# Emitting the weight conversion of the first batch by sums of engine times

## The chip, the cores and the metric

The kernel runs on one core of one Trainium2 chip. The metric is the device time of one execution in microseconds (us). Before the change it is 1535.84 us, the median of three runs (1533.26 to 1537.35).

## What is computed

The reference, cut to what matters (float32 tensors of attention; the four weight matrices arrive as float64):

```python
def sm_attn(qq, kk, vv):
    s = scale * np.matmul(qq, kk.transpose(0, 1, 3, 2))
    a = np.exp(s - np.max(s, axis=-1, keepdims=True))
    return np.matmul(a / (np.sum(a, axis=-1, keepdims=True) + 1e-09), vv)
# q, k, v: (8, 8, 576, 64); p: (8, 8, 32, 64)
p_packed = sm_attn(p, k, v)
out = sm_attn(q, p_packed, p_packed)
x = out.transpose(0, 2, 1, 3).reshape(4608, 512)
h = x @ w_in                      # (512, 2048)
x = (h - np.tanh(h)) @ w_out      # (2048, 512)
r = np.maximum(x @ w_in2, 0.0)
out = (s * (r * r) + b) @ w_out2
```

## The kernel before, in words

The attention and the first MLP run batch by batch; the second MLP follows and is not touched. For each batch the packed keys give z, which is the attention's last product folded into w_in: one z per column block c of 512 of w_in (four blocks, `make_z`, L421), and a, the softmax of the second attention, one per half of the batch's tokens (`second_stage`, L624). A step j is one of 16 blocks of 128 rows of d_ff: `mm1` (L456) multiplies z by a for block j, `act_pe` or `act1` forms h - tanh(h), and `mm2` (L492) adds the product with row block j of w_out. Numbers are split into a high and a low float32r part, so each product is three matmuls. The first batch goes in four parts of eight steps j: half 0 and half 1 with j from 0 to 7, then both halves with j from 8 to 15. Its first three parts use `act_pe`, which keeps the subtraction of tanh on TensorE; the fourth and all later batches use `act1`, which does it on VectorE.

The weights are converted from float64 to float32 on the chip during the first batch. `to_f32` (L114) does it in five instructions: an absolute value on ScalarE (L119), a clamp, a shift and two bit merges on VectorE (L121, L123, L126, L129). `w1_steps(c, i)` converts half i of column block c of w_in (128 x 1024 numbers). `wo1_steps(j)` converts row block j of w_out (128 x 512), and then splits it: a cast on ScalarE (L138) and a subtraction (L140), on GpSimd for j below 12, else on VectorE. Each is a generator that yields after each instruction.

Every engine works its own instructions in the order in which the program emits them, and DMAs wait in the queue of the engine that issues them. The order is made by hand. `first_weights` (L687) lists groups of generators; `in_turn` (L634) runs the groups one after another, the members of one group in turns (`both`, L527), and starts the generators of the next group after 13 steps of a group, or four for each of its members if that is fewer. `attention` (L777) goes on from there with the attention of the next batches. `slot` (L806) is called at six places of a step j, between matmuls, and takes steps out of that generator: before the last row block of w_out is converted, 5, 3, 4 or 1 sixths of a step in the four parts (SLOTS), and after each `mm1` 6, 5, 4 or 1 more (AFTER). After that it is one step a slot, and four more a step j (CATCH_UP) until a of batch 1 is there. `until` (L648) takes steps until something that the next instruction needs has been emitted: z before `mm1`, row block j before `mm2`.

Loads of float64 weights go out on SyncE's queue (SP). `load_wo1` (L586) puts row blocks 8 to 11 into the place of blocks 4 to 7, so each waits for the subtraction of one of these; a column block's load waits for a free one of nine large buffers (`take_turn`, L561). The loads of k, v and q of batch 1 and later are issued by GpSimd (`load_k` L161, `load_v` L173, `load_q` L231): 16, 2 and 16 DMAs; those of k and q have pieces of 128 bytes, 288 in each DMA. `second_loads` (L629) issues the first of them. `load_p` (L226) is on SP. A second generator (`second_weights`, L703) converts the weights of the second MLP later on, a step every third slot.

Of the kernel before, what the change touches and what calls it, by code (L numbers as in the profile page):

```python
# [18 lines left out]
def pack_attention_two_mlps(ctx, tc, q, k, v, p, w_in1, w_out1, w_in2, w_out2, s_in, b_in, out):  # L19
# [36 lines left out]
    AFTER, SLOTS = (6, 5, 4, 1), (5, 3, 4, 1)  # L56
    ON_PE = 3
    AHEAD, CATCH_UP, FIRST_W = 13, 4, range(23, 33)
# [55 lines left out]
    def to_f32(x, src, t):  # L114


        low, high = words(src)
        tf = t.bitcast(F32)
        nc.scalar.activation(tf, high.bitcast(F32), AF.Abs)  # L119
        yield  # L120
        nc.vector.tensor_scalar(out=tf, in0=tf, scalar1=EXP_LO, scalar2=EXP_HI, op0=ALU.max, op1=ALU.min)  # L121
        yield
        nc.vector.tensor_scalar(out=t, in0=t, scalar1=3, scalar2=0x3FFFFFF8, op0=ALU.logical_shift_left,  # L123
                                op1=ALU.bitwise_and)
        yield
        nc.vector.scalar_tensor_tensor(out=t, in0=high, scalar=-0x40000000, in1=t, op0=ALU.bitwise_and,  # L126
                                       op1=ALU.bitwise_or)
        yield
        nc.vector.scalar_tensor_tensor(out=x.bitcast(I32), in0=low, scalar=29, in1=t,  # L129
                                       op0=ALU.logical_shift_right, op1=ALU.bitwise_or)  # L130
        yield
# [29 lines left out]
    def load_k(b, g):  # L161
        for hp in range(2):
            h0 = 4 * g + 2 * hp
            t = apool.tile([P, 2, C, 32], F32, tag="kr", name=f"k_{b}_{g}_{hp}", bufs=2)
            rows = k[b, h0:h0 + 2].rearrange("h (r a n) d -> a r h n d", a=2, n=C)
            for a in range(2):
                for u in range(2):
                    p0 = (2 * a + u) * 32
                    for e in range(2):
                        nc.gpsimd.dma_start(out=t[p0:p0 + 32, e], in_=rows[a][:, e, :, u * 32:u * 32 + 32])  # L170
            k_t[b, g, hp] = t

    def load_v(b, g):  # L173

        t = apool.tile([P, 4, CT * D], F32, tag="v", name=f"v_{b}_{g}", bufs=1)
        src = v[b, 4 * g:4 * g + 4].rearrange("h (r c) d -> r h (c d)", c=C)
        nc.gpsimd.dma_start(out=t[:R], in_=src[:, :, :CT * D])
        nc.gpsimd.dma_start(out=t[R:, :, :(C - CT) * D], in_=src[:, :, CT * D:])
        v_t[b, g] = t.rearrange("r h (c d) -> r h c d", c=CT)
# [51 lines left out]
    def load_q(b, hf):  # L231
        for g in range(G):
            for hp in range(2):
                h0 = 4 * g + 2 * hp
                t = apool.tile([P, HB // 32, 32], F32, tag="qr", name=f"q_{b}_{hf}_{g}_{hp}", bufs=4)
                for u in range(2):
                    for e in range(2):
                        src = q[b, h0 + e, hf * HB:(hf + 1) * HB, u * 32:u * 32 + 32]
                        p0 = (2 * e + u) * 32
                        nc.gpsimd.dma_start(out=t[p0:p0 + 32], in_=src.rearrange("(n r) d -> r n d", r=32))  # L240
# [286 lines left out]
    def both(gens):  # L527
        gens = list(gens)
        while gens:
            for g in list(gens):  # L530
                try:
                    next(g)
# [3 lines left out]
                yield  # L536
# [14 lines left out]
    with tc.manual_schedule():  # L551
# [82 lines left out]
        def in_turn(*groups):  # L634

            groups = [[call_late(g) for g in group] for group in groups]
            for n, group in enumerate(groups):
                for i, _ in enumerate(both(group)):
                    yield
                    if i == min(AHEAD, 4 * len(group)) and n + 1 < len(groups):  # L640
                        for g in groups[n + 1]:
                            next(g)

        def call_late(f):
            g, *a = f
            yield from g(*a)

        def until(key, gen):  # L648
            forced.append(key)
            while key not in done:  # L650
                next(gen)
# [35 lines left out]
        def first_weights():  # L687
            yield from in_turn(
                [(w1_steps, 1, 0)], [(w1_steps, 1, 1)],
                [(wo1_steps, 0), (wo1_steps, 1)],  # L690
                [(first_z, 1), (wo1_steps, 2), (wo1_steps, 3)],
                [(wo1_steps, 4), (wo1_steps, 5)],
                [(second_stage, 0, 1), (wo1_steps, 6), (wo1_steps, 7)],
                [(w1_steps, 2, 0)], [(w1_steps, 2, 1)],
                [(wo1_steps, 8), (wo1_steps, 9)],
                [(first_z, 2), (wo1_steps, 10), (wo1_steps, 11)],
                [(w1_steps, 3, 0)], [(w1_steps, 3, 1)],
                [(wo1_steps, 12), (wo1_steps, 13), (second_loads,)],
                [(first_z, 3), (wo1_steps, 14), (wo1_steps, 15)])
# [106 lines left out]
        def slot():  # L806
# [20 lines left out]
        for b in range(B):  # L827
# [4 lines left out]
            for hf, js in parts:  # L832
# [10 lines left out]
                for j in js:  # L843
# [14 lines left out]
                    if on_pe:  # L858
                        next(t)
                    between = None  # L860
# [453 lines left out]
```

## Time and profile before

| what | value |
|---|---|
| median of three runs | 1535.84 us |
| the profiled execution | 1534.77 us, of which the span from first to last instruction is 1533.0 us |
| granted clock of TensorE, mean | 0.986 |
| busy, share of the span | TensorE 96%, its weight loads 91%, VectorE 70%, ScalarE 49%, GpSimd 24% |
| first batch, its four parts | 45.7, 34.8, 29.3 and 33.0 us |

Parts are cut at the first `mm1` of each. In the table a busy TensorE includes time in which a matmul stands in its pipeline; the weight loads are the closer measure of its pace. A wait in the trace is the idle time of an engine ahead of an instruction, with what ended it.

### The profile page before, as it was taken

How to read it: one execution, taken by the hardware profiler on the slowest of the kernel's cores; microseconds unless marked ns; L12 is line 12 of the kernel's file. 1: busy time of each engine (PE TensorE's matmuls, PEld its weight loads, DVE VectorE, ACT ScalarE, POOL GpSimd, SP SyncE). 2: the span in 40 equal slices, each digit the busy share in tenths (PEclk: the TensorE clock that was granted, in tenths of full speed). 3: DMA queues.
4: the chain of work that ended last, by engine and by line, in shares of the span. 5: the costliest groups of instructions: out<-in, count | busy, mean ns of one | idle time of the engine just before them, and what ended most of it. 6: DMA issues, size and time to landing. Idle time of an engine off the chain costs nothing.

```text
span 1533.0 us, 28189 instructions
## 1 busy us (share of the span) xinstructions
PE 1473.5 (96%) x10548; PEld 1387.5 (91%) x10548; DVE 1066.9 (70%) x2032; ACT 756.7 (49%) x1466; POOL 368.8 (24%) x584
## 2 busy tenths in 40 slices
PE   6689899999999999999999999999998999999998
PEld 3578698998988989888999999999998999999998
DVE  4784887878787797876554777777776865565563
ACT  3465344544444444443334656656666655454442
POOL 0238462534527275543001000000031000000000
PEclk8799999999999999999999999999999999999999
DMA  9656454554634444342427465465498886676673
GB/s 211 195 144 156 109 151 124 141 145 125 169 95 129 114 133 124 86 108 81 157 90 297 173 245 225 177 257 215 186 317 322 251 252 185 220 239 195 222 236 83
DMA packets 250394, 271.64 MB, mean 177 GB/s; under 512 B 113040, under 2 KB 188816, under 8 KB 250256
## 3 DMA queue, kind: packets, MB, share of 16 engines
q1 hardware_dynamic: 226880, 222.42, 45.3%
q0 software_dynamic: 22848, 46.83, 11.5%
q8 instruction: 83, 1.36, 0.4%
q10 hardware_dynamic: 528, 0.59, 0.1%
q14 instruction: 55, 0.45, 0.1%
HBM read 161.61 MB, written 108.13 MB: 176 GB/s over the span
## 4 chain that ended last, share of the span: by engine, by line
PE 82%; DVE 8%; DMA 3%; ACT 2%; issue 2%; SPq 1%; POOL 1%; ACTq 0%; DVEq 0%; POOLq 0%
PE acc L499 21%; PE h L464 11%; PE Y L1252 10%; PE Y L1035 9%; PE Z L1252 7%; PE X L1035 6%; PE X L1252 6%; PE Z L1035 6%; PE zp L367 2%; DMA w1s<-in_moe_w_in_dram 1%; SPq L194 1%; DVE gl L135 1%; DMA wo1s<-in_moe_w_out_dram 1%; PE pv L339 1%; PE s L270 1%
## 5 line engine op out<-in xcount | busy, mean ns | idle before, releaser
L499 PE MATMUL acc<-gh,wo 128*128 128x288 f32 x2040 | 419.7, 297 | 4.3 <-POOL wo L140 4.3
L499 PEld LDWEIGHTS acc<-gh,wo 128*128 128x128 f32 x2040 | 330.7, 189 | 4.6 <-POOL wo L140 4.5
L499 PE MATMUL acc<-gl,wo 128*128 128x288 f32 x1020 | 310.1, 304 | 6.7 <-ACT wo L138 2.8
L472 ACT ACTIVATE t<-h 128x288 f32<-128x288 f32 x232 | 95.3, 411 | 299.7 <-PE h L464 255.6
L499 PEld LDWEIGHTS acc<-gl,wo 128*128 128x128 f32 x1020 | 193.1, 189 | 33.9 <-issue 18.7
L464 PE MATMUL h<-a2h,z 128*128 128x288 f32 x1024 | 214.7, 297 | 1.5 <-ACT z L445 1.5
L939 DVE TENSOR_TENSOR x<-B,x 128x768 fp32r<-128x768 f32 x158 | 147.2, 950 | 82.8 <-ACT x L1186 68.0
L473 DVE TENSOR_TENSOR t<-h,t 128x288 f32<-128x288 f32 x232 | 104.2, 449 | 135.5 <-ACT t L472 134.8
L464 PE MATMUL h<-a2l,z 128*128 128x288 f32 x512 | 161.0, 314 | 8.8 <-ACT gl L483 3.4
L464 PEld LDWEIGHTS h<-a2h,z 128*128 128x128 f32 x1024 | 165.7, 190 | 2.9 <-ACT z L445 1.7
L240 POOL DMA_DIRECT2D q<-in_q_dram x224 | 135.2, 612 | 133.0 <-DVE qT L374 113.7
L1035 PE MATMUL Y<-x,w 128*128 128x384 f32 x864 | 160.6, 339 | 4.8 <-DVE g L939 4.1
L1035 PEld LDWEIGHTS Y<-x,w 128*128 128x128 f32 x864 | 152.9, 190 | 5.5 <-DVE g L939 4.4
L1252 PE MATMUL Y<-x,w 128*128 128x384 f32 x864 | 153.2, 335 | 0.7 <-DVE s L939 0.7
L1252 PEld LDWEIGHTS Y<-x,w 128*128 128x128 f32 x864 | 150.3, 188 | 1.0 <-DVE s L939 1.0
L170 POOL DMA_DIRECT2D k<-in_k_dram x224 | 136.1, 615 | 50.2 <-DVE kT L290 40.7
L464 PEld LDWEIGHTS h<-a2l,z 128*128 128x128 f32 x512 | 97.7, 191 | 26.3 <-issue 6.8
L1186 ACT CAST x<-B 128x768 fp32r<-128x768 f32 x116 | 94.0, 833 | 47.1 <-DMA B<-g 30.6
L1035 PE MATMUL X<-x,w 128*128 128x384 f32 x576 | 108.0, 336 | 0.0
L1035 PE MATMUL Z<-x,w 128*128 128x384 f32 x576 | 107.9, 336 | 0.0
L135 DVE TENSOR_TENSOR gl<-t,gh 128x288 fp32r<-128x288 f32 x231 | 107.0, 463 | 0.0
L1252 PE MATMUL X<-x,w 128*128 128x384 f32 x576 | 102.6, 336 | 0.0
(176 smaller groups left out, 2269.6 us busy)
## 6 DMA issues: line engine op xcount, KB each, us to landing
g<-g SPq DMA_DIRECT2D x196, 384.0 KB, 3.5
B<-g SPq DMA_DIRECT2D x116, 384.0 KB, 4.5
w<-w_d POOLq DMA_DIRECT2D x28, 512.0 KB, 6.0
B<-x2t SPq DMA_DIRECT2D x24, 384.0 KB, 5.7
g<-s SPq DMA_DIRECT2D x24, 384.0 KB, 2.8
out_dram<-g SPq DMA_DIRECT2D x192, 48.0 KB, 1.8
x2t<-xs SPq DMA_DIRECT2D x15, 576.0 KB, 3.7
w1s<-in_moe_w_in_dram SPq DMA_DIRECT2D x32, 256.0 KB, 8.2
```

Of the source, the lines that this page charges most:

```text
L135: (eng or nc.vector).tensor_tensor(out=lo, in0=x, in1=hi.bitcast(F32), op=ALU.subtract)
L170: nc.gpsimd.dma_start(out=t[p0:p0 + 32, e], in_=rows[a][:, e, :, u * 32:u * 32 + 32])
L240: nc.gpsimd.dma_start(out=t[p0:p0 + 32], in_=src.rearrange("(n r) d -> r n d", r=32))
L367: nc.tensor.matmul(ps[e][i * M:(i + 1) * M, :rhs(i).shape[-1]], pblk[b][r, h // 4, h % 4 * M:h % 4 * M + M], rhs(i)[r], start=True, stop=True)
L464: nc.tensor.matmul(h[:, :HB], zt[:, zi, g, f0:f0 + P], a[:, g], start=(n == 0), stop=(n == 3 * G - 1))
L472: nc.scalar.activation(t, h[:, :HB], AF.Tanh)
L473: nc.vector.tensor_tensor(out=t, in0=h[:, :HB], in1=t, op=ALU.subtract)
L499: nc.tensor.matmul(acc[m][:, :HB], w[:, m * P:(m + 1) * P], x, start=(j == js[0] and i == 0), stop=(j == js[-1] and i == 2))
L939: self.nc.vector.tensor_tensor(out=o, in0=a, in1=b, op=op)
L1035: self.nc.tensor.matmul(bank[:, f, :self.TH], w[:, f, a, kt], x[:, b, kt], start=(p in ("P1", "P5", "P6") and m == 0), stop=(m == 5), skip ...
L1186: self.nc.scalar.copy(self.xs[(7 * self.NBK + n) % self.XS][:, 0], self.ready[0])
L1252: nc.tensor.matmul(bank[:, ft, :T], w[:, kk, u, ft], x[:, v, kk], start=first and p in ("P1", "P5", "P6"), stop=last, skip_group_check=True)
```

## The change

Every yield of `to_f32` now gives a number, an estimate of the time on VectorE; a yield without one counts as half a STEP (0.17). Two sums are kept: `clock[0]` grows by SLOT with every slot, `clock[1]` by what is emitted, and a slot emits until the second is ahead of the first by LEAD. AFTER, SLOTS, AHEAD and CATCH_UP go. This goes on until a of batch 1 is emitted, so it paces the first attention steps of batch 1 too; after that it is one step a slot. A group takes the first step (the absolute value) of the next group's conversions when each of its members has had a step. The order of groups is changed: row blocks 0 to 3 of w_out stand ahead of column block 1 of w_in; z(1) goes with row blocks 4 and 5; `second_loads` goes from the group of row blocks 12 and 13 to its own place ahead of column block 2. The loads of k, v and q of batch 1 are issued on SP instead of GpSimd.

```diff
-    AFTER, SLOTS = (6, 5, 4, 1), (5, 3, 4, 1)
+    STEP, SLOT, LEAD = 0.34, (0.7, 0.52, 0.52, 0.42), 1.0
-    AHEAD, CATCH_UP, FIRST_W = 13, 4, range(23, 33)
+    FIRST_W = range(23, 33)
...
+        one = STEP * (len(t.shape) - 1)
         nc.scalar.activation(tf, high.bitcast(F32), AF.Abs)
-        yield
+        yield 0.0
...
-        yield
+        yield one
...
-        yield
+        yield 2 * one
...
-                        nc.gpsimd.dma_start(out=t[p0:p0 + 32, e], in_=rows[a][:, e, :, u * 32:u * 32 + 32])
+                        (nc.gpsimd if b > 1 else nc.sync).dma_start(out=t[p0:p0 + 32, e], in_=rows[a][:, e, :, u * 32:u * 32 + 32])
...
         def in_turn(*groups):
 
-            groups = [[call_late(g) for g in group] for group in groups]
+            groups = [[(f, f(*a)) for f, *a in group] for group in groups]
             for n, group in enumerate(groups):
-                for i, _ in enumerate(both(group)):
-                    yield
-                    if i == min(AHEAD, 4 * len(group)) and n + 1 < len(groups):
-                        for g in groups[n + 1]:
-                            next(g)
+                for i, cost in enumerate(both([g for _, g in group])):
+                    yield cost
+                    if i == len(group) and n + 1 < len(groups):
+                        for f, g in groups[n + 1]:
+                            if f in (w1_steps, wo1_steps):
+                                next(g)
+
+        clock = [0.0, 0.0]
+
+        def step(gen):
+            cost = next(gen)
+            clock[1] += STEP / 2 if cost is None else cost
 
         def until(key, gen):
             forced.append(key)
-            while key not in done:
-                next(gen)
+            if key not in done:
+                while key not in done:
+                    step(gen)
+                clock[0] = max(clock[0], clock[1])
             forced.pop()
...
-                [(w1_steps, 1, 0)], [(w1_steps, 1, 1)],
-                [(wo1_steps, 0), (wo1_steps, 1)],
-                [(first_z, 1), (wo1_steps, 2), (wo1_steps, 3)],
-                [(wo1_steps, 4), (wo1_steps, 5)],
+                [(wo1_steps, 0)], [(wo1_steps, 1)],
+                [(wo1_steps, 2), (wo1_steps, 3)],
+                [(w1_steps, 1, 0)], [(w1_steps, 1, 1)],
+                [(first_z, 1), (wo1_steps, 4), (wo1_steps, 5)],
                 [(second_stage, 0, 1), (wo1_steps, 6), (wo1_steps, 7)],
+                [(second_loads,)],
                 [(w1_steps, 2, 0)], [(w1_steps, 2, 1)],
-                [(wo1_steps, 8), (wo1_steps, 9)],
-                [(first_z, 2), (wo1_steps, 10), (wo1_steps, 11)],
+                [(first_z, 2), (wo1_steps, 8), (wo1_steps, 9)],
+                [(wo1_steps, 10), (wo1_steps, 11)],
                 [(w1_steps, 3, 0)], [(w1_steps, 3, 1)],
-                [(wo1_steps, 12), (wo1_steps, 13), (second_loads,)],
-                [(first_z, 3), (wo1_steps, 14), (wo1_steps, 15)])
+                [(first_z, 3), (wo1_steps, 12), (wo1_steps, 13)],
+                [(wo1_steps, 14), (wo1_steps, 15)])
...
-            if ("wo", NF - 1) not in done:
-                n = SLOTS[part[0]]
-                for _ in range(ticks[0] * n // 6 - (ticks[0] - 1) * n // 6):
-                    next(fill)
+            if ("wo", NF - 1) in done and ticks[0] % 3 == 1:
+                next(more, None)
+            if ("a", 1, 0) in done:
+                next(fill, None)
                 return
-            if ticks[0] % 3 == 1:
-                next(more, None)
-            next(fill, None)
+            clock[0] += SLOT[part[0]]
+            while clock[1] <= clock[0] + LEAD and ("a", 1, 0) not in done:
+                step(fill)
...
-                    if ("wo", NF - 1) not in done:
-                        for _ in range(AFTER[part[0]]):
-                            next(fill)
-                    elif ("a", 1, 0) not in done:
-                        for _ in range(CATCH_UP):
-                            next(fill)
...
                     if on_pe:
                         next(t)
+                    else:
+                        clock[1] += 2 * STEP
```

The same choice of queue stands in `load_v` (two DMAs) and `load_q`; `both` hands the numbers through.

## Rows read from the trace of the kernel before

**Rows 1.** The page: its first line, and part 1.

```profile
span 1533.0 us, 28189 instructions
...
PE 1473.5 (96%) x10548; PEld 1387.5 (91%) x10548; DVE 1066.9 (70%) x2032; ACT 756.7 (49%) x1466; POOL 368.8 (24%) x584
```

**Rows 2.** Busy time by stage: parts 0 to 3 of the first batch, and a later stretch.

```profile
core 0: us, PE busy (x) PEld busy (x) DVE busy (x) ACT busy (x) POOL busy (x), PEclk, DMA share, GB/s
39.00:84.70 45.70, 33.44 (x177) 26.93 (x177) 32.80 (x58) 23.27 (x49) 14.01 (x8) 0.78 0.59 182
84.70:119.50 34.80, 29.50 (x202) 24.14 (x203) 32.46 (x45) 21.63 (x47) 15.17 (x19) 1.00 0.57 149
119.50:148.80 29.30, 28.88 (x252) 25.73 (x253) 13.32 (x32) 16.22 (x45) 26.57 (x45) 1.00 0.72 173
148.80:181.80 33.00, 29.54 (x272) 22.01 (x271) 23.96 (x62) 13.73 (x38) 16.66 (x28) 1.00 0.44 113
190.00:310.00 120.00, 119.58 (x1073) 109.67 (x1073) 99.97 (x267) 57.10 (x154) 61.41 (x102) 1.00 0.53 142
```

**Rows 3.** DVE in order of time: start us, us, line, tiles, count [idle before].

```profile
51.38 0.76 DVE L121 TENSOR_SCALAR t<-t 128x512 f32<-128x512 f32 x2
...
53.92 1.29 DVE L129 SCALAR_TENSOR_TENSOR wo1s<-wo1s,t 128x512 int32<-128x512 int32 x2
64.21 0.43 DVE L121 TENSOR_SCALAR t<-t 128x512 f32<-128x512 f32 x1 [9.00 <-ACT t L119]
```

**Rows 4.** DVE in order of time, from second_stage(0,1) to column block 3.

```profile
70.42 0.47 DVE L389 STREAM_TRANSPOSE t<-s 128x288 f32<-128x288 f32 x1
...
85.75 0.69 DVE L121 TENSOR_SCALAR w<-w 128x1024 f32<-128x1024 f32 x1
...
87.20 1.23 DVE L126 SCALAR_TENSOR_TENSOR w<-w1s,w 128x1024 int32<-128x1024 int32 x1
88.46 1.22 DVE L129 SCALAR_TENSOR_TENSOR w<-w1s,w 128x1024 int32<-128x1024 int32 x1
...
104.69 0.69 DVE L121 TENSOR_SCALAR w<-w 128x1024 f32<-128x1024 f32 x1 [1.12 <-ACT w L119]
...
107.18 2.22 DVE L126 SCALAR_TENSOR_TENSOR w<-w1s,w 128x1024 int32<-128x1024 int32 x1
```

**Rows 5.** PE in order of time: mm1 (h), z's products (zp), scores (s).

```profile
66.69 0.40 PE L464 MATMUL h<-a2h,z 128*128 128x288 f32 x1 [1.51 <-ACT z L445]
...
92.48 2.17 PE L367 MATMUL zp<-w,pblk 64*32 64x512 f32 x16
...
119.50 0.40 PE L464 MATMUL h<-a2l,z 128*128 128x288 f32 x1 [0.92 <-ACT gl L483]
...
125.40 0.51 PE L464 MATMUL h<-a2l,z 128*128 128x288 f32 x1
...
167.96 0.71 PE L367 MATMUL s<-qT,pblk 64*32 64x288 f32 x14 [0.78 <-DVE z L435]
...
180.15 1.69 PE L367 MATMUL zp<-w,pblk 64*32 64x512 f32 x16 [2.46 <-DVE z L435]
```

**Rows 6.** ACT in order of time: absolute values, and the first Exp of stage1.

```profile
63.50 1.24 ACT L119 ACTIVATE t<-wo1s 128x512 f32<-128x512 f32 x2
...
103.53 1.13 ACT L119 ACTIVATE w<-w1s 128x1024 f32<-128x1024 f32 x1
...
134.77 0.41 ACT L310 ACTIVATE e<-s,nm 128x160 f32<-128x160 f32 x1 [1.89 <-DVE nm L302]
```

**Rows 7.** SP's queue in order of time: issues of DMAs, us from first to last.

```profile
72.00 10.44 SPq L594 DMA_DIRECT2D wo1s<-in_moe_w_out_dram  x4
82.49 5.78 SPq L148 DMA_DIRECT2D w1s<-in_moe_w_in_dram  x8
...
1222.78 3.92 SPq L1218 DMA_DIRECT2D out_dram<-g  x8
```

**Rows 8.** Issues at 30.7 to 31.2, 82.3 to 82.9 and 196 to 206: KB each, us to landing.

```profile
wo1s<-in_moe_w_out_dram SPq DMA_DIRECT2D x1, 512.0 KB, 9.4
...
w1s<-in_moe_w_in_dram SPq DMA_DIRECT2D x1, 256.0 KB, 6.5
...
k<-in_k_dram POOLq DMA_DIRECT2D x3, 36.0 KB, 3.6
```

More of the change, by code (lines that the diff above doesn't have):

```diff
@@ L118, in to_f32 @@
         tf = t.bitcast(F32)
+        one = STEP * (len(t.shape) - 1)
         nc.scalar.activation(tf, high.bitcast(F32), AF.Abs)
-        yield
+        yield 0.0
         nc.vector.tensor_scalar(out=tf, in0=tf, scalar1=EXP_LO, scalar2=EXP_HI, op0=ALU.max, op1=ALU.min)
-        yield
+        yield one
         nc.vector.tensor_scalar(out=t, in0=t, scalar1=3, scalar2=0x3FFFFFF8, op0=ALU.logical_shift_left,
                                 op1=ALU.bitwise_and)
-        yield
+        yield one
         nc.vector.scalar_tensor_tensor(out=t, in0=high, scalar=-0x40000000, in1=t, op0=ALU.bitwise_and,
                                        op1=ALU.bitwise_or)
-        yield
+        yield 2 * one
         nc.vector.scalar_tensor_tensor(out=x.bitcast(I32), in0=low, scalar=29, in1=t,
                                        op0=ALU.logical_shift_right, op1=ALU.bitwise_or)
-        yield
+        yield 2 * one
     def split(hi, lo, x, eng=None):
@@ L176, in load_v @@
         src = v[b, 4 * g:4 * g + 4].rearrange("h (r c) d -> r h (c d)", c=C)
-        nc.gpsimd.dma_start(out=t[:R], in_=src[:, :, :CT * D])
-        nc.gpsimd.dma_start(out=t[R:, :, :(C - CT) * D], in_=src[:, :, CT * D:])
+        (nc.gpsimd if b > 1 else nc.sync).dma_start(out=t[:R], in_=src[:, :, :CT * D])
+        (nc.gpsimd if b > 1 else nc.sync).dma_start(out=t[R:, :, :(C - CT) * D], in_=src[:, :, CT * D:])
         v_t[b, g] = t.rearrange("r h (c d) -> r h c d", c=CT)
@@ L239, in load_q @@
                         p0 = (2 * e + u) * 32
-                        nc.gpsimd.dma_start(out=t[p0:p0 + 32], in_=src.rearrange("(n r) d -> r n d", r=32))
+                        (nc.gpsimd if b > 1 else nc.sync).dma_start(out=t[p0:p0 + 32], in_=src.rearrange("(n r) d -> r n d", r=32))
                 q_t[b, hf, g, hp] = t
@@ L531, in both @@
                 try:
-                    next(g)
+                    cost = next(g)
                 except StopIteration:
@@ L535, in both @@
                     continue
-                yield
+                yield cost
     def seq(*gens):
@@ L634, in in_turn @@
         def in_turn(*groups):
-            groups = [[call_late(g) for g in group] for group in groups]
+            groups = [[(f, f(*a)) for f, *a in group] for group in groups]
             for n, group in enumerate(groups):
-                for i, _ in enumerate(both(group)):
-                    yield
-                    if i == min(AHEAD, 4 * len(group)) and n + 1 < len(groups):
-                        for g in groups[n + 1]:
[L642 to L646, printed above, removed]
+                for i, cost in enumerate(both([g for _, g in group])):
+                    yield cost
+                    if i == len(group) and n + 1 < len(groups):
[6 more added lines that the diff above has]
+            clock[1] += STEP / 2 if cost is None else cost
         def until(key, gen):
             forced.append(key)
-            while key not in done:
-                next(gen)
+            if key not in done:
+                while key not in done:
+                    step(gen)
+                clock[0] = max(clock[0], clock[1])
             forced.pop()
```

## The prediction

> **What bounds the kernel now.** I read the page first: the span is 1533.0 us and TensorE (PE) is busy for 96% of it [rows 1]. The busy time by stage then shows where the rest is [rows 2]. I cut the first batch into its four parts of eight steps j (a part is one half of the tokens with eight of the sixteen blocks of d_ff). From 190 us on PE is busy for 119.58 of 120 us, and no planner of conversions runs there; an edit of the first batch can only shift that. The four parts take 45.7, 34.8, 29.3 and 33.0 us. The first two have PE idle for 12.3 and 5.3 us, with VectorE (DVE) busy for 32.80 and 32.46 us: in part 1 that is 93%. So parts 0 and 1 go at the pace of the weight conversion on DVE. Part 2 is PE's (28.88 of 29.3), with DVE busy for 13.32 only. In part 3 PE is idle for 3.46 us, and its weight loads are busy for 22.01 us, where the share of the steady stretch (109.67 of 120) would give 30.2: some 8.1 us of PE's pace are lost there.
>
> Two rows name the loss in part 0. DVE stands for 9.00 us before the clamp of rows 4 and 5 of w_out1, until ScalarE (ACT) has done their absolute value [rows 3]; ACT does it at 63.50 [rows 6], as it works in order and had the casts of earlier steps j before it, which waited for PE. And PE waits for z(1)'s second half before the fifth step j, which goes on at 66.69 [rows 5].
>
> **The order that the change makes.** A step costs what the new code says: 2.38 for a row block of w_out1 (2.04 for DVE, two steps of 0.17), 4.08 for a half of w_in1, 0.17 for any other step. A slot adds 0.7 in part 0 and 0.52 in parts 1 and 2, with 1.0 of lead; a step j has six slots. At the fifth j of part 0 z(1) is forced: by then blocks 0 to 3, both halves of w_in1's column block 1, z(1) and blocks 4 and 5 are out, 24.2 in all, and the clock is set to that. The group of second_stage(0,1) with blocks 6 and 7 takes 9.0, second_loads 0.7, column block 2 8.2: 42.1. Part 0 ends at 24.2 + 4 x 4.2 = 41.0. So column block 2 is out when part 1 begins, and z(2)'s products are emitted inside its first mm1; before, they stood in its third step j, at 92.48 [rows 5]. All conversions (72.7) are out at the second j of part 2, the same place as before.
>
> **Part by part.**
>
> (1) Parts 0 and 1. Blocks 0 and 1 now go ahead of column block 1. Block 0's load, issued at 30.8, lands 9.4 us later [rows 8], at 40.2; with its absolute value (half of 1.24 [rows 6]) DVE begins at 40.8. A pair of blocks takes from 51.38 to 55.21 on DVE, 3.83 us [rows 3]; a half of w_in1 from 85.75 to 89.68, 3.9 [rows 4]. Two pairs, 7.7, give 48.5; column block 1, 7.8, gives 56.3. GpSimd's (POOL's) subtractions for blocks 1 to 3 now run beside it, and one of them made a step of DVE 2.22 long in place of 1.23 [rows 4]: 3 x 1.0, so 59.3. Then z(1)'s products, two casts, and behind the casts of blocks 4 and 5 in ACT's order its second halves: 65.5 to 66.5, against 66.69. The 9.00 us of standing are used, but by work that came earlier before; PE gains nothing here, and DVE is two blocks further on.
>
> From there the group of second_stage(0,1) took from 70.42 to 85.75 [rows 4]. It now begins behind the half of mm1 at about 66.5, with the first step of its two blocks done (0.8) and its absolute values ahead (about 1.5 of waits, an estimate from those rows' gaps): 13.0 us, so column block 2 begins at 79.5, 6.2 us earlier, and is done at 87.3. But PE has z(2)'s products in its queue there, some 7 us after it began part 1: it stands. Then it has 9.7 steps j to the third j of part 2. Two steps take 119.50 to 125.40, 2.95 each [rows 5]: 28.6. To this come z(2)'s and z(3)'s products and corrections (2.7), two evictions at part ends (0.8 each half hidden, 0.8), and the clock: part 0, where PE stood in several places, ran at 0.78 on average, every later part at 1.00 [rows 2], so I put 2.7 for a stretch of 6 us at 1.2 GHz after the stop. 87.3 + 34.8 = 122.1; with 0.7 for the xs copies, which DVE now does when PE is late, 122.8 against 125.40: **-2.6**. Bounds: -6.2 (PE follows DVE all the way) and 0.
>
> (2) second_loads moves ahead of column block 3 and from POOL's queue to SP's. That is 2 + 16 + 2 + 16 issues. SP issued w_out1's blocks 8 to 11 from 72.00 to 82.44 and column block 3 right behind, from 82.49 [rows 7]; blocks 10 and 11 wait for POOL's blocks 6 and 7, now 6.2 earlier, so SP reaches second_loads at 76.3. No row shows k or q with 128-byte pieces on SP. The nearest is the store of the output, 384 pieces each: eight in 3.92 us, 0.49 [rows 7]. For 288 pieces I take 0.42, between 0.37 (in proportion) and 0.49: 15.1 us, to 91.4. Column block 3's first half: four issues (1.7), 6.5 to landing [rows 8], its absolute value 1.13 [rows 6]: 100.8, against the start of its DVE steps at 104.69 before [rows 4]. It is no later than (1) needs: **0**, bounds 0 and the first rival's. The Trainium skill, "DMA: Bandwidth & Descriptors", section "Issuing engines are not separate DMA queues", says that DMAs of all issuing engines run on the same 16 DMA engines, and that issuing on several only saves the sequencer's time. By that rule the move frees no transfer and gives up a second issuer: it would be a loss of whatever SP's line costs, and nothing else.
>
> (3) The attention of batch 1 up to a(1,0) is some 127 steps. Before, a step j gave ten (six slots and CATCH_UP), so 60 in the rest of part 2 and the others through 6.7 steps j of part 3. Now a slot of part 2 gives 0.52 / 0.17, three, so 18 in a step j and 111 in part 2; 1.5 steps j of part 3 are left. Its DVE work falls into part 2, where DVE has 16 us free. Of the 8.1 us lost in part 3 the wait before z(3) of batch 1 (2.46, the product at 180.15 [rows 5]) stays, as that needs part 3's own steps, and 1.0 is for products with small weights that cost no pace: **-4.6**, bounds -8.1 and 0.
>
> What is late next is in part 2. Between the scores and the transposes of stage1 stand 13 steps, 1.3 steps j before, 0.7 now (2.1 us). ACT stood 1.89 us for DVE in it even before [rows 6], with the four Exp to follow; I put 1.0 for each of two stages: **+2.0**. The 16 loads of k(1,1), now on SP, take 16 x 0.42 + 3.6 [rows 8] = 10.3 us, and the 42 steps up to their use 2.3 steps j with the attention's own products, about 10: nothing, bounds 0 and +4. The bounds of the whole are 0 and +6.
>
> POOL's queue loses the loads of batch 1 and only keeps its subtractions; nothing on the path waits for it. The w2 conversion starts in the same place. Costs of the planner are in no engine's time.
>
> Sum: -2.6 + 0 - 4.6 + 2.0 = **-5.2 us**. It is made against the profiled execution (1534.77, its span 1533.0), which lies 1.1 under the median; I take it off the median: 1535.84 - 5.2 = **1530.6**.
>
> **Rivals.**
>
> A, slower: SP's line decides. If an issue takes c, column block 3's first half starts 36c - 18.8 from where it did (76.3 + 36c + 1.7 + 6.5 + 1.13 against 104.69 gives 36c - 19.0; 0.2 is for gaps), ACT stands with it, as its absolute value is queued a group ahead, and so does PE. The k loads add 16(c - 0.42). The gain is gone at 36c - 18.8 + 16(c - 0.42) = 2.6, c = 0.54. Under load SP's eight issues of column block 3 took 5.78, 0.72 each, part of it waiting for the buffer [rows 7]. At 0.63, half way from 0.54 to that, the terms are +3.9 - 4.6 + 2.0 + 3.4 = +4.7: 1540.5. For it: second_loads runs beside 1 MB of blocks 10 and 11. Against: its DMAs have 288 pieces or fewer where those of 0.49 us have 384. Chance 0.21. It is also what the rule cited above would give.
>
> B, no change: part 3 does not recover, since its pace is set by act1 and the z of batch 1 on DVE, not by second_stage. Then -2.6 + 0 + 2.0, 1535.2. For it: the waits of 0.78 and 2.46 are both for z's subtraction [rows 5]. Chance 0.30.
>
> C, a larger gain: PE follows DVE in part 1 (-5.4) and part 3 loses nothing more (-7.1), with +2.0: 1525.3. Chance 0.17.
>
> The forecast has 0.32.
>
> **How the numbers follow.** A measurement of this kernel can tell about 0.3%, 4.6 us, from no change. The forecast lies just beyond it, so a part of its chance is counted as the same: faster 0.46 (C, nine tenths of the forecast), same 0.31 (B and the edge of the forecast and of A, less B's edges), slower 0.23 (A and the bounds of (3)). The range runs from 1521.5 (C with the remaining bounds of (1)) to 1540.5 (A).
>
> **What would show it.** DVE without the 9 us gap; column block 2 at 79.5 and its z(2) product in part 1's first step with PE standing before it; SP's second_loads from about 76 to 91, column block 3's DVE steps at about 101; the third j of part 2 at 122.8; part 3 near 28 us. I am wrong if column block 3 starts after 105, or if part 2 grows by more than part 3 shrinks.

## The result, and the profile after

The changed kernel takes 1550.22 us (median of 4 runs, 1549.34 to 1550.51), the kernel before 1534.95 beside it on the same chip (4 runs, 1533.26 to 1537.35). The ratio is 1.0097 with a 95% interval of [1.008, 1.0115]: slower by 15 us, where 1530.6 was forecast. The profiled execution took 1550.51 us, its span is 1548.7, against 1533.0 before. The page of the changed kernel, its first line and busy times, which answer to [rows 1]:

```profile
span 1548.7 us, 28215 instructions
...
PE 1482.3 (96%) x10548; PEld 1391.3 (90%) x10548; DVE 1063.2 (69%) x2032; ACT 758.4 (49%) x1466; POOL 325.6 (21%) x516
```

The work is the same; it takes longer. Busy time by stage in the changed kernel, each part cut at its own first mm1, and a later stretch, as in [rows 2]:

```profile
core 0: us, PE busy (x) PEld busy (x) DVE busy (x) ACT busy (x) POOL busy (x), PEclk, DMA share, GB/s
36.87:88.32 51.45, 36.80 (x193) 26.71 (x194) 44.74 (x72) 26.00 (x52) 12.48 (x8) 0.74 0.67 189
88.32:122.53 34.21, 27.95 (x188) 25.07 (x187) 20.42 (x30) 20.21 (x45) 5.73 (x4) 0.90 0.73 177
122.53:170.68 48.15, 41.47 (x347) 29.92 (x345) 22.85 (x55) 20.14 (x60) 11.07 (x18) 0.93 0.48 98
170.68:192.67 21.99, 21.99 (x177) 19.86 (x178) 16.45 (x43) 11.12 (x26) 0.00 (x0) 1.00 0.34 101
200.00:320.00 120.00, 118.79 (x1047) 108.33 (x1047) 97.53 (x262) 57.83 (x154) 57.22 (x96) 1.00 0.52 141
```

In the kernel before, part 3's first mm1 is at 148.41, 0.4 us ahead of the cut of [rows 2]; counted from there part 2 took 28.9 and part 3 33.4 us. Part 3 shrinks to 22.0 us, far more than the 4.6 of term (3), but most of that is work which moved: part 2 now holds 347 matmuls for 252, part 3 177 for 272. Part 2 grows to 48.15: 6.7 us of it PE idle, and its clock at 0.93 of full speed where it was 1.00. Part 0 ends 3.6 us later (88.32 for 84.72): z(2)'s products now stand ahead of part 1's first mm1, and the granted clock was 0.60 from 80 to 84 us, behind a stop of 2.15 us.

The points that the prediction cut the time at, in the two profiled executions (us):

| | before | after | change | forecast |
|---|---|---|---|---|
| third step j of part 2, from the span's start | 125.40 | 130.09 | +4.7 | -2.6 |
| the same, from part 0's first mm1 (39.03, 36.87) | 86.4 | 93.2 | +6.9 | |
| from there to part 3 | 23.0 | 40.6 | +17.6 | +2.0 |
| part 3 | 33.4 | 22.0 | -11.4 | -4.6 |
| batch 1 to the end of the span | 1351.2 | 1356.0 | +4.8 | 0 |

The second row is the better measure of the first. The start of part 0 is no effect of the change: it differs between executions of the same order (36.47 to 39.95 us in the kernel before and three variants of it that part from it only later), and in the changed kernel's profiled execution it came 2.2 us earlier than in the other. From that point to the third j the granted clock is 0.82 on average where it was 0.88, and from the third j to batch 1 it is 0.95 where it was 1.00. By an estimate from these rows (the busy time of PE times the share of the clock that is missing) that is some 4 us of the 6.9, and 3 us of the 6.2 that the next two rows come to. PE also stands 3.9 and 2.3 us longer there.

DVE in the changed kernel, which answers to [rows 3, 4]: the copies of x at the end of part 0, the first conversion steps of column blocks 2 and 3, the split of row block 12, and the transposes of k(1,1) in part 2.

```profile
79.10 0.69 DVE L122 TENSOR_SCALAR w<-w 128x1024 f32<-128x1024 f32 x1 [0.55 <-ACT w L120]
...
93.85 0.46 DVE L100 COPY xs<-acc 128x288 f32<-128x288 f32 x1 [3.20 <-PE acc L500]
...
104.43 0.69 DVE L122 TENSOR_SCALAR w<-w 128x1024 f32<-128x1024 f32 x1 [4.01 <-ACT w L120]
...
122.65 0.69 DVE L141 TENSOR_TENSOR wo<-cv,wo 128x512 fp32r<-128x512 f32 x1 [4.05 <-ACT wo L139]
...
142.89 0.84 DVE L291 STREAM_TRANSPOSE kT<-k 128x288 f32<-128x288 f32 x2 [2.86 <-DMA k<-in_k_dram]
146.17 0.48 DVE L291 STREAM_TRANSPOSE kT<-k 128x288 f32<-128x288 f32 x1 [2.45 <-DMA k<-in_k_dram]
```

The 9.00 us gap of [rows 3] is gone, and column block 2 starts at 79.10, where 79.5 was forecast. Then the lead is lost: column block 3 starts at 104.43, as in [rows 4] (104.69). At the copies of x, column block 3, the split and the transposes DVE stood 0.5, 1.1, 0.4 and 2.4 us in the kernel before.

SP's queue in the changed kernel, which answers to [rows 7]; behind the time of the first issue stands the time to the end of the last:

```profile
65.87 8.76 SPq L595 DMA_DIRECT2D wo1s<-in_moe_w_out_dram  x4
74.68 0.94 SPq L230 DMA_DIRECT2D pc<-in_p_dram  x2
75.66 10.37 SPq L171 DMA_DIRECT2D k<-in_k_dram  x16
...
87.44 8.59 SPq L241 DMA_DIRECT2D q<-in_q_dram  x16
96.08 3.74 SPq L149 DMA_DIRECT2D w1s<-in_moe_w_in_dram  x8
...
132.00 0.56 SPq L518 DMA_DIRECT2D x2t<-xs  x1
135.33 0.53 SPq L523 DMA_DIRECT2D xp<-x2t  x1
135.91 9.09 SPq L171 DMA_DIRECT2D k<-in_k_dram  x16
```

second_loads holds SP from 74.68 to 96.03: 36 issues, 0.59 us each on average (0.65 for k, 0.54 for q), where 0.42 was taken. Of the 32 issues for k and q 25 took 0.44 to 0.47 us, one every 0.50; what raises the mean is a few long ones (1.46 and 0.80 us) and waits: at 80.11 and 91.71 SP goes on when the DMA that it issued eight before has landed. Column block 3's loads go out at 96.08. And k(1,1) stands behind the store of part 1's x and the reload of part 0's, which cannot go before that store's tile is free: 135.91.

What stands behind these loads, ACT and PE in part 1 and in part 2 of the changed kernel:

```profile
103.28 1.12 ACT L120 ACTIVATE w<-w1s 128x1024 f32<-128x1024 f32 x1 [6.17 <-DMA w1s<-in_moe_w_in_dram]
104.74 0.61 PE L465 MATMUL h<-a2l,z 128*128 128x288 f32 x1 [6.01 <-ACT gl L484]
...
146.71 2.06 PE L271 MATMUL s<-kT,ppT 64*32 64x288 f32 x8 [2.25 <-DVE kT L291]
149.99 0.41 ACT L311 ACTIVATE e<-s,nm 128x160 f32<-128x160 f32 x1 [6.97 <-DVE nm L303]
```

ACT stands 6.17 us at an absolute value queued a group ahead, with the casts of the step j behind it in its order, and PE stands 6.01 for one of these. The step j behind that stop takes 4.40 us at a granted clock of 0.62, where the next two, at 1.00, take 3.0 and 3.3. In part 2 the chain is longer: the load of k, DVE's transposes, PE's scores, DVE's maxima, and ACT 6.97 us before the first Exp.

### The profile page after: what moved, and what is told of

Read it like the earlier page. It is cut to its first block, busy times and chain, and to the rows that moved or that the text cites. A ratio compares the mean times of both kernels' runs of the same rounds, so it can differ in the third digit from the quotient of the medians.

```text
span 1548.7 us, 28215 instructions
## 1 busy us (share of the span) xinstructions
PE 1482.3 (96%) x10548; PEld 1391.3 (90%) x10548; DVE 1063.2 (69%) x2032; ACT 758.4 (49%) x1466; POOL 325.6 (21%) x516
## 4 chain that ended last, share of the span: by engine, by line
PE 79%; DVE 6%; DMA 5%; issue 4%; SPq 2%; POOL 2%; ACT 2%; DVEq 0%; ACTq 0%; POOLq 0%
PE acc L500 21%; PE h L465 10%; PE Y L1255 10%; PE Y L1038 9%; PE Z L1255 6%; PE X L1255 6%; PE X L1038 6%; PE Z L1038 6%; PE zp L368 2%; SPq L195 1%; DMA w1s<-in_moe_w_in_dram 1%; PE s L271 1%; DVE gl L136 1%; DMA g<-g 1%; POOL k L171 1%
## 5 line engine op out<-in xcount | busy, mean ns | idle before, releaser
L241 POOL DMA_DIRECT2D q<-in_q_dram x192 | 115.5, 610 | 155.8 <-DVE qT L375 154.0
L171 POOL DMA_DIRECT2D k<-in_k_dram x192 | 116.1, 612 | 81.6 <-DVE kT L291 38.9
L1189 ACT CAST x<-B 128x768 fp32r<-128x768 f32 x116 | 94.0, 833 | 47.0 <-DMA B<-g 28.9
```

The source lines that it names most:

```text
L171: (nc.gpsimd if b > 1 else nc.sync).dma_start(out=t[p0:p0 + 32, e], in_=rows[a][:, e, :, u * 32:u * 32 + 32])
L241: (nc.gpsimd if b > 1 else nc.sync).dma_start(out=t[p0:p0 + 32], in_=src.rearrange("(n r) d -> r n d", r=32))
L1189: self.nc.scalar.copy(self.xs[(7 * self.NBK + n) % self.XS][:, 0], self.ready[0])
```

## The experiments

Three things might cost the 15 us: the queue and place of batch 1's loads (theory Q), the pace of the attention in part 2 (P), and the order of the conversions. Each was taken back or done alone. Ratios are to the kernel before on the same chip, with 95% intervals. "Third j" is the start of part 2's third step j, "stretch" the time from there to batch 1's first mm1, in the profiled execution; before they are 125.4 and 56.4, after 130.1 and 62.6. The third j holds the 2 to 3 us by which part 0's start differs between executions; the section on the account gives it without them.

### First set: queue, place and pace

**pool_loads**: the loads of batch 1 on GpSimd again (also in `load_v` and `load_q`).

```diff
-                        (nc.gpsimd if b > 1 else nc.sync).dma_start(...)
+                        nc.gpsimd.dma_start(...)
```

> The changed kernel with the loads of k, v and q of batch 1 issued by GpSimd again, all else as changed. Theory Q (SP's line costs it: second_loads ahead of column block 3, and k(1,1) behind the store and reload of x in part 2): column block 3's loads are issued at about 77 us, its DVE steps start at about 92, part 1 gives back the 5 to 7 us that it lost, k(1,1) is there in time and part 2 shrinks from 48.2 to 33 us or less; 1530 to 1535 us. Rival P (the pace: three steps of attention a slot leave too little work between an engine's result and its user in part 2): part 1 gives back the same 5 us, part 2 stays at 43 us or more; 1543 to 1547 us.

Measured 1550.38 us, 1.0096 [1.0074, 1.0118]; third j 130.0, stretch 59.8. A miss for both. Column block 3 is earlier (its DVE steps begin at 99.75, though not at 92), but part 1 loses as much in another place. GpSimd's queue, DVE, SP's queue, ACT and PE in this kernel:

```profile
94.93 8.25 POOL L241 DMA_DIRECT2D q<-in_q_dram  x13 [0.55 <-DMA k<-in_k_dram]
...
104.00 5.09 POOL L141 TENSOR_TENSOR wo<-wo1s,wo 128x512 fp32r<-128x512 f32 x4
...
103.67 5.99 DVE L122 TENSOR_SCALAR w<-w 128x1024 f32<-128x1024 f32 x1
...
109.12 0.36 SPq L595 DMA_DIRECT2D wo1s<-in_moe_w_out_dram  x1
...
112.70 0.68 ACT L120 ACTIVATE t<-wo1s 128x512 f32<-128x512 f32 x1 [5.69 <-DMA wo1s<-in_moe_w_out_dram]
113.72 0.61 PE L465 MATMUL h<-a2l,z 128*128 128x288 f32 x1 [5.57 <-ACT gl L484]
```

The same 34 DMAs now hold GpSimd until 104.00, with the subtractions of row blocks 8 to 11 behind them. Row block 13's load waits for block 11's place, ACT for that load (5.69 us), PE for ACT (5.57). The four subtractions in a row also meet a clamp of DVE: it lasts 5.99 us beside them, where the one before it in this form takes 0.74.

**loads_late**: second_loads back behind column block 3, still on SP.

```diff
-                [(second_loads,)],
...
-                [(first_z, 3), (wo1_steps, 12), (wo1_steps, 13)],
+                [(first_z, 3), (wo1_steps, 12), (wo1_steps, 13), (second_loads,)],
```

> The changed kernel with second_loads, still on SP, back in the group of row blocks 12 and 13, behind column block 3's loads. Only the first place of theory Q goes away: column block 3's DVE steps at about 92 in place of 104.4, the third step j of part 2 at 124 to 126 in place of 130.1; k(1,1) still stands behind the store and reload of x. By theory Q and by rival P part 2's stalls stay, so 1543 to 1546 us; if all of the loss hangs on the late column block 3, 1530 to 1533.

Measured 1549.30 us, 1.0094 [1.0078, 1.011]; third j 127.0, stretch 64.8. The third j recovers 3.1 us (4.9 counted from part 0's start; column block 3's DVE steps begin at 102.18, not at 92), and the stretch behind it loses 2.2 of them again: k(1,1) goes out at 135.55, behind the store and the reload as in the changed kernel, and DVE stands 5.18 and 3.38 us for it. A miss by 3 us for both theories, as neither took in that part 2 would give the gain back.

**slow_pace**: the old pace after the last conversion.

```diff
+            if ("wo", NF - 1) in done:
+                next(fill, None)
+                return
             clock[0] += SLOT[part[0]]
...
                     h = mm1(b, hf, j, slot)
+                    if ("wo", NF - 1) in done and ("a", 1, 0) not in done:
+                        for _ in range(4):
+                            next(fill)
```

> The changed kernel, but once row block 15 is converted the attention of batch 1 goes at the old pace (one step a slot and four after each mm1) until a of batch 1. SP's line is left as it is. Rival P: part 2's stalls go, 48.2 us becomes 34 (the late column block 3 stays), part 3 takes 31 in place of 22: 1543 to 1546 us. Theory Q: k(1,1) is emitted later and still stands behind the store and reload of x, part 2 and 3 together stay within 3 us of the 70 us they take now: 1547 to 1552.

Measured 1543.77 us, 1.0053 [1.0034, 1.0071]; third j 130.7, stretch 57.4. As P expected, not Q: 5.2 us of the stretch come back, and parts 2 and 3 together take 65.0 us for 70.1.

**before_on_sp**: the kernel before with the loads of batch 1 on SP.

```diff
-                        nc.gpsimd.dma_start(...)
+                        (nc.gpsimd if b > 1 else nc.sync).dma_start(...)
```

> The kernel before with one thing changed: the loads of k, v and q of batch 1 are issued on SP. second_loads stands there behind column block 3's loads, so part 1 is as before. Theory Q: what is left of it is k(1,1) behind the store and reload of x and the w2 loads behind that; 1538 to 1543 us. Rival P: the pace is the old one, so 1535, no change.

Measured 1542.62 us, 1.0045 [1.0028, 1.0062]; third j 125.5, stretch 63.2. As Q expected. The loss starts in one place; DVE and PE in this kernel, at k(1,1):

```profile
146.76 0.93 DVE L290 STREAM_TRANSPOSE kT<-k 128x288 f32<-128x288 f32 x2 [5.15 <-DMA k<-in_k_dram]
...
151.34 0.84 DVE L290 STREAM_TRANSPOSE kT<-k 128x288 f32<-128x288 f32 x2 [3.65 <-DMA k<-in_k_dram]
151.87 1.53 PE L270 MATMUL s<-kT,ppT 64*32 64x288 f32 x8 [3.45 <-DVE kT L290]
```

In the kernel before GpSimd issued these 16 loads from 132.1 to 143.7; DVE waited 2.4 us for them and PE not at all. The first and the last of GpSimd's rows there:

```profile
132.11 5.03 POOL L170 DMA_DIRECT2D k<-in_k_dram  x8
...
140.10 3.60 POOL L170 DMA_DIRECT2D k<-in_k_dram  x6 [0.72 <-DMA k<-in_k_dram]
```

and SP's in before_on_sp:

```profile
132.76 0.56 SPq L517 DMA_DIRECT2D x2t<-xs  x1
136.19 0.57 SPq L522 DMA_DIRECT2D xp<-x2t  x1
...
139.31 10.17 SPq L170 DMA_DIRECT2D k<-in_k_dram  x16
```

On SP they go out from 139.31 to 149.48, behind the store at 132.76 and the reload at 136.19. PE is idle for 8.15 us of the stretch where it was for 3.88, and the granted clock over it is 0.97 where it was 1.00; together these are most of the 6.8 us.

So Q and P both hold. The second set takes them apart.

### Second set: what is left when both are undone

**late_pool**: pool_loads and loads_late together.

> The changed kernel with second_loads back in the group of row blocks 12 and 13 and the loads of batch 1 back on GpSimd: what stays of the change is the pace, the order of the other groups and the absolute values a group ahead. If SP's and GpSimd's lines were all that is wrong, 1533 to 1536 us. Theory P (pace of the attention in part 2): part 2 begins at 119 to 120 as before, parts 2 and 3 together take 67 us in place of 62.3, and 3 to 4 us more go in batches 1 to 7: 1542 to 1545 us.

Measured 1542.80 us, 1.0051 [1.0031, 1.0071]; third j 125.3, stretch 61.3. As P expected in time; parts 2 and 3 took 68.9 us for 67.

**late_pool_slow**: late_pool with the edit of slow_pace.

> As the kernel before it, and the old pace (one step a slot and four after each mm1) once row block 15 is converted. What is left of the change is the planner of the conversions, their order and the absolute values a group ahead. Theory P: parts 2 and 3 take 62 to 64 us, and only the 3 to 4 us in batches 1 to 7 are left: 1537 to 1540 us. If it takes 1543 or more, the loss of the kernel before it was not the pace.

Measured 1537.51 us, 1.0011 [0.9995, 1.0027]; third j 126.4, stretch 58.0. As P expected in time (parts 2 and 3 took 65.6 us, 1.6 more than expected), and not distinguishable from the kernel before. PE's and DVE's waits from 119 us on, one row each from late_pool (in all, times, longest; windows to 193 and 160 us):

```profile
PE s L271 <- DVE kT L291: 3.2, 3, 2.4
...
DVE kT L291 <- DMA k<-in_k_dram: 5.7, 3, 2.8
```

and the same from late_pool_slow:

```profile
PE s L271 <- DVE kT L291: 0.3, 1, 0.3
...
DVE kT L291 <- DMA k<-in_k_dram: 4.5, 2, 2.4
```

DVE waits for k in both. PE is idle for 6.8 us of the stretch in the first and for 3.8 in the second, a difference of 3.0, nearly all of it this wait. At ten steps a step j the scores stand far enough behind in PE's order that PE hardly sees it; at eighteen PE stands.

**before_fast**: the kernel before at the new pace.

```diff
-    AHEAD, CATCH_UP, FIRST_W = 13, 4, range(23, 33)
+    AHEAD, CATCH_UP, FIRST_W = 13, 12, range(23, 33)
```

> The kernel before with one thing changed: CATCH_UP = 12 in place of 4, so that the attention of batch 1 goes at 18 steps a step j instead of 10 until a of batch 1. Conversions, queues and the phase of the second MLP's weights are as before. Theory P: part 2 loses more than part 3 wins, 1538 to 1541 us. Rival (the pace is worth what the prediction's term (3) says, -4.6 + 2.0): 1532 to 1533 us.

Measured 1547.73 us, 1.0066 [1.0046, 1.0086]; third j 122.7, stretch 69.4. P, and more than expected: 13 us in the stretch. Half of these are PE's: it is idle for 10.4 us where it was for 3.9. Most of the other half is the clock: 0.90 on average over the stretch, 1.00 before. Of PE's waits 3.8 us are for k's transposes and 2.9 for an addition of x on DVE. DVE and ACT in this kernel:

```profile
139.17 0.84 DVE L290 STREAM_TRANSPOSE kT<-k 128x288 f32<-128x288 f32 x2 [4.23 <-DMA k<-in_k_dram]
...
145.57 0.41 ACT L310 ACTIVATE e<-s,nm 128x160 f32<-128x160 f32 x1 [7.22 <-DVE nm L302]
```

**land16**: the changed kernel with the conversion of the second MLP's weights two of its steps later.

```diff
-    LAND = 14
+    LAND = 16
```

> The changed kernel with LAND = 16 in place of 14, so that the conversion of the second MLP's weights, which starts six slots earlier since the change (row block 15 is emitted at slot 99 rather than 104), stands against the batches as before. Theory T (this phase costs the 3 to 5 us that are lost after batch 0): 1545 to 1547 us. Rival (they are lost otherwise): 1549 to 1551 us.

Measured 1550.53 us, 1.0084 [1.0058, 1.0109]; 1550.22 without the edit, at another time. The time is the rival's, and theory T isn't borne out; but T's 1545 to 1547 us are about 1.0065 to 1.0079 of the kernel before, inside the interval, so it isn't excluded either. From batch 1 on this kernel and before_fast give PE, DVE and ACT the same instructions in the same order, yet from batch 1's first mm1 to SP's last store of x the profiled executions take 605.0 and 599.2 us. Windows around the largest of the steps by which they part, of land16:

```profile
490.00:500.00 10.00, 7.75 (x57) 7.27 (x56) 2.80 (x8) 3.77 (x14) 8.77 (x14) 0.98 0.28 60
500.00:510.00 10.00, 9.03 (x84) 8.69 (x85) 6.71 (x21) 2.79 (x9) 2.73 (x5) 0.68 0.57 148
```

and of before_fast:

```profile
490.00:500.00 10.00, 7.42 (x89) 6.77 (x88) 3.55 (x12) 4.13 (x15) 7.00 (x12) 1.00 0.46 121
500.00:510.00 10.00, 10.00 (x87) 9.29 (x86) 8.47 (x21) 3.51 (x10) 6.60 (x12) 1.00 0.51 132
```

After a short stop of PE in the same place (3.2 us idle in land16's two windows, 2.6 in before_fast's) the granted clock fell to 0.68 of full speed in one and stayed at 1.00 in the other. Some us after batch 0 hang on this and can't be laid to the change from one execution.

### Third set: can the rest be won

**lps_no_ahead**: late_pool_slow, without an absolute value ahead for row blocks 12 and 13.

```diff
-                            if f in (w1_steps, wo1_steps):
+                            if f in (w1_steps, wo1_steps) and a[0] not in (12, 13):
```

> As late_pool_slow, but the absolute values of row blocks 12 and 13 are no longer taken a group ahead. Row block 13's load goes out only when GpSimd is done with row block 11. Theory L (ACT stands in order for that load, and PE behind it): the step of 6.4 us from the sixth to the seventh j of part 1 becomes 3.1 to 4, part 2 begins at 115.5 to 117 in place of 118.8, and 2 to 3 us of that are left at the end: 1534.5 to 1536 us. Rival (the conversions on DVE set the place of the third j of part 2 whatever ACT does): the third j stays at 126 and the time at 1537 to 1538.

Measured 1537.48 us, 1.0022 [1.0009, 1.0035]; third j 125.6, stretch 56.6. Theory L falls, the rival holds: the step from the sixth to the seventh j of part 1 stays at 6.4 us. PE's waits from 36 to 130 us in this kernel, the first row:

```profile
PE zp L368 <- DVE w L130: 10.5, 4, 4.7
```

The products of z stand 10.5 us for the converted blocks. In the kernel before this wait is 0.2 us, and PE stands for the conversion elsewhere: 4.3 us for GpSimd's split of a row block, 2.8 for ACT's, 2.5 for DVE's copies of x. In all PE is idle for 17.5 us from part 0's first mm1 to the third j in the kernel before, and for 16.6 in this one. That it is DVE's pace which is paid either way is an inference; no run took it apart.

**lps_xs_act**: the same, with batch 0's copies of x all on ACT.

```diff
-                evac(xs[:, m], acc[m][:, :HB])
+                (nc.scalar.copy if b == 0 else evac)(xs[:, m], acc[m][:, :HB])
```

> As the kernel before it, and batch 0's four copies of x at the end of a part are all made by ACT, none by DVE. At the end of part 0 DVE stood 3.3 and 0.9 us for PE at the two copies it had, with the clamps of column block 3's first half behind them in its order. Theory L: DVE's conversions come 3 to 5 us earlier from there, and the third j of part 2 2 to 3 us earlier than in the kernel before it: 1532 to 1534 us. Rival (ACT then stands at the copies and holds up the casts and absolute values by as much): no change against the kernel before it.

Measured 1541.65 us, 1.0046 [1.003, 1.0062]; third j 127.8, stretch 56.1. A miss for theory L, and slower than its rival: ACT comes to the copies at 97.32 only, behind its casts, and to column block 3's absolute value at 98.77; DVE stands 4.96 us for that.

**late_pool_gap**: late_pool, with 30 empty steps ahead of the second stage1.

```diff
                 yield from stage1(b + 1, 0, (b + 1, 1), (b + 1, 1))
+                yield from wait(30 if b == 0 else 0)
```

> As late_pool (new pace), with 30 empty steps, ten slots, between the two stage1 of batch 1, so that DVE asks for k(1,1) some 5 us later. In late_pool DVE stood 2.84 and 2.65 us for its loads and PE 0.57 and 2.45 behind it. If that wait is most of what the pace costs: 1538 to 1540 us. If the pace costs by the short distances between an engine's result and its user in all of stage1 and z: at most 3 us of the 7 to 8 come back, 1540 to 1543 us.

Measured 1540.64 us, 1.0043 [1.0028, 1.0057]; third j 126.7, stretch 57.1. In the stretch 4.2 of late_pool's 4.9 us come back, and PE's wait for k's transposes falls from 3.2 us to 0.2. Its third j came 1.3 us later in that execution, though, and of the total 1 to 2 us come back, within what the intervals leave open; by the expected times it lies with the second theory. In that stretch PE's wait for k(1,1) is most of what the pace costs. The empty steps also slow the attention as a whole (part 3 takes 28.9 us for late_pool's 22.0), so this run alone doesn't separate the two theories, and why less is left at the end isn't settled.

**before_slow**: the kernel before with fewer steps.

```diff
-    AHEAD, CATCH_UP, FIRST_W = 13, 4, range(23, 33)
+    AHEAD, CATCH_UP, FIRST_W = 13, 2, range(23, 33)
```

> The kernel before with CATCH_UP = 2 in place of 4, eight steps of the attention of batch 1 in a step j rather than ten; the other end of before_fast. If the distance between result and user is what costs, part 2 gains up to 2 us and part 3 loses some, as a of batch 1 is there only eight slots before its use: 1533 to 1538 us. A clear loss (1540 or more) would say that the attention of batch 1 is the path in part 3, and that the old pace was near its best.

Measured 1536.63 us, 1.0021 [1.0007, 1.0035]; third j 124.7, stretch 54.3. Slightly slower, but not where the expectation had it: PE stands 3.9 us for a of batch 1, which comes too late, and even so the stretch is 2.1 us shorter than before. What is lost lies behind batch 1's first mm1 (1358.1 us to the end for 1351.2, in the profiled executions), and no run says why. In time the old pace is near its best on both sides; no version tried beats the kernel before.

### The account

The four kernels with either pace and with second_loads early on SP or late on GpSimd add up. In percent over the kernel before: 0.97 with both changes, 0.53 without the pace, 0.51 without the queue and place, 0.11 without both. The pace costs 0.44 or 0.40% (6.8 or 6.1 us), queue and place 0.46 or 0.42% (7.1 or 6.4 us), what is left 0.11% (1.7 us, not distinguishable from nothing); each of these is uncertain by some 0.2 to 0.3%, as the intervals show. Place and queue are not two costs that add: early on SP, early on GpSimd and late on SP all come to 0.94 to 0.97% at the new pace, for three different waits, shown above. Only late on GpSimd, where the loads stood before, is cheaper. The pace alone in the old order costs 0.66% [0.46, 0.86] in before_fast, not clearly more. Of the pace's cost the stretch shows 5.1 us between the changed kernel and slow_pace and 3.3 between late_pool and late_pool_slow; where the rest lies isn't shown.

Counted from part 0's first mm1, so that its start drops out, the third j comes after 85.5 to 86.4 us in the kernel before, before_on_sp, before_fast and before_slow; after 85.9 to 88.2 in late_pool, late_pool_slow, lps_no_ahead and late_pool_gap; after 88.3 in loads_late, 90.4 in lps_xs_act and 91.8 in pool_loads; and after 92.3 to 93.2 in slow_pace, land16 and the changed kernel. Executions of one order thus differ by some 2 us here, and the early place of second_loads costs 4 to 7.

## Why the prediction was wrong

**(1) Parts 0 and 1, -2.6.** In late_pool, where neither SP's nor GpSimd's line disturbs part 1, the third j is at 125.35: 0, not -2.6, and counted from part 0's start the kernels with this order are no earlier than the kernel before, as above. DVE's first half went as worked out: column block 2 started at 79.10 in the changed kernel and at 78.39 in late_pool, for 79.5. The step that failed is where PE stands when that block is done, the "9.7 steps j" behind 87.3. z(2)'s products were emitted a step j earlier than worked out, not in part 1's first mm1 but in part 0's last step. PE in late_pool:

```profile
86.23 1.93 PE L368 MATMUL zp<-w,pblk 64*32 64x512 f32 x8 [2.70 <-DVE w L130]
...
89.53 0.56 PE L465 MATMUL h<-a2l,z 128*128 128x288 f32 x1
```

PE waits 2.70 us for the second half of column block 2 there, and part 0's last step takes 9.54 us for 3.41 before, so part 1 begins at 89.53 with all ten steps j still to go. Those take 35.8 us, about what was put down (34.8 + 0.7), with PE idle for 1.7; what was gained in part 1 was lost ahead of it. The changed kernel lost more, behind the late loads of term (2): its part 1 ran at a granted clock of 0.90 and part 2 at 0.93, beyond the 2.7 us that were put down for the clock here.

**(2) second_loads on SP, 0.** It failed in its price: c is 0.59, not 0.42. The row of the store [rows 7] gave 0.49 for 384 pieces, and I went below it toward the proportion of the pieces; the loads of 288 pieces went out one every 0.50, like the stores, and SP's waits for earlier DMAs came on top. By rival A's formula 0.59 gives 36 x 0.59 - 18.8 = +2.4 for the third j; counted from part 0's start it was +6.9, with the stands and the lower clock that follow. It also failed in what it took for the alternative: pool_loads shows that the early place is no better on GpSimd, whose subtractions stand behind the issues.

**(3) The attention pulled into part 2, -4.6.** Part 3 gave back more than that, 11.4 us, but "what is late next", +2.0, was +17.6 in the changed kernel, so that this term is +6.2 in sum, not -2.6; before_fast alone has +13, half of it at the lower clock, which had no term here. I priced distances between DVE and ACT and called the loads of k(1,1) "nothing", with a bound of +4, by comparing issue time with the steps ahead of their use. Two things were left out: that they are queued behind a store and a reload, which SP can't issue before 132.0 and 135.3, and that PE's scores are emitted at the same faster pace, so that PE meets DVE's wait for k. Even GpSimd, as fast as before, is then too late (DVE stood 5.7 us for them in late_pool, PE 3.2).

**Rivals.** A had the sign and the place: SP's line. Its price for queue and place, 3.9 + 3.4 = 7.3 us at c = 0.63, is close to what was measured, 6.4 to 7.1, though partly by luck: at the 0.59 that was measured the same formula gives 5.1, and column block 3, which it puts later, started no later than before (104.43 for 104.69). It kept -4.6 + 2.0 for the pace, where +6 to +7 stands, so its 1540.5 was 10 us short. B and C were wrong on the pace too. The signs named for being wrong: column block 3 did not start after 105, as the absolute values ahead passed its lateness to ACT and PE instead; part 2 did grow by more than part 3 shrank. The low end of the range, 1521.5, isn't what it is called: C with the remaining bounds of (1) would be 1524.5, and 1521.5 takes the bounds of (1) and (3) without the +2.0.

The Trainium skill, "DMA: Bandwidth & Descriptors", section "Issuing engines are not separate DMA queues", says that several issuers save only the sequencers' time. before_on_sp agrees that nothing is won by the move, 1.0045. But what the second issuer saved here was the place in the line, not issue time: at k(1,1) SP's line carried a store and a reload that wait for other work, and GpSimd's did not.

**The later 4.8 us** had no term. How much of it is the change's stays open. The ratio makes the whole loss 14.9 us, and 13.1 of them are there at batch 1's first mm1 when counted from part 0's start, which leaves 2. Executions with the same order behind batch 1's start differ by more: 599.2 us to SP's last store of x in before_fast and 605.0 in land16. In the kernel before it is 598.6, in the changed one 603.5. Over the whole of it PE is idle for 22.4 us before and 23.0 after, and the granted clock is 1.00 in both.

## What to carry to other kernels

Before moving a run of DMAs to another queue or place, write down what is queued behind each on the issuing engine, and ahead of it what it waits for: a load behind a store inherits that store's wait. In this kernel a faster emission of side work paid only up to the point where its consumers met the latency of its loads; count the distance on the engine that is the bound, not on the one that waits first. Work taken ahead stands in its engine's order too: an absolute value queued a group ahead held the casts behind it for 6.17 us until its load had landed. And before two profiled executions are compared at a point, subtract what differed ahead of the change.

## What was not expected of the hardware

The time of an issue didn't go with the pieces: loads of 288 pieces of 128 bytes took 0.45 us each on SP in the median, one every 0.50, like the stores with 384 pieces [rows 7] (median 0.47); on GpSimd it was 0.61, one every 0.63 (8.25 for 13). In the changed kernel's second_loads SP also waited, for 1.0 and 0.7 us, for the landing of the DMA issued eight before. A clamp of 128x1024 on DVE lasted 5.99 us beside four subtractions on GpSimd (pool_loads), and the one before it 0.74. And with the same order of instructions a short stop of PE in the same place was followed by a granted clock of 0.68 in one profiled execution and of 1.00 in another.
